# Turned tiles with PSUM banks of their own, wider turned blocks, and a new written order

## The chip, the cores and the metric

One core of one Trainium2 chip. The metric is the device time of one launch in microseconds (us), as the median of several runs; lower is better. The granted clock of TensorE was 1.00 of its upper level (2.4 GHz) in all but the last stretch of the profiled execution, where it was 0.98. Engines: PE (matrix engine), DVE (vector), ACT (scalar), POOL (GpSimd), SP (issues DMAs).

## The reference

Two sequences of 768 tokens go through three stages, all in fp32.

```
# 1. retention, 8 heads of 64, gamma_h = 1 - 2^(-5-h)
state = gamma * state + k_t v_t^T ;  y_t = q_t state / 8
# 2. layer norm and MLP, with residual, width 512 -> 2048 -> 512
xn = (x - mean) / sqrt(var + 1e-6) * g_ln
x  = x + relu(xn @ w_ch1) @ w_ch2
# 3. four experts' causal attention, head size 64
q, k, v = x @ wq[e], x @ wk[e], x @ wv[e]
a = softmax(causal(q k^T / 8));  ye = a @ v @ wo[e]
out = sum over the 2 experts with the largest x @ w_gate, softmax weight * ye
```

## The kernel before

**Tiles.** Retention works on 12 tiles of 128 tokens (2 sequences by 6). A tile needs: scores (`r_tile 2`, L581), the masked scores `am` on DVE (L587), the product with the old state (L600) and with the own values (L610), the update of the state in PSUM (L618), the scaling into `xT` in SBUF (DVE, L630), a turn of `xT` by eight 64x64 transposes against `ident` (`turn`, L422), statistics of that turned tile on DVE (L642 to L644) and POOL (L650, L651), the normed tile `xn` on ACT (L655), a second turn of `xn` (L422), and its copy on ACT (L664). The MLP works on stretches of 384 tokens. Each fp32 operand is split into a rounded high part and a low part, and a product takes three passes (high by high, high by low, low by high). First products stand at L766 and L858, second ones at L788; the residual is added into `xT` by DVE (L794, `m_c 2`). The last addition of a block is made in place in PSUM (L798, `m_c 3`), and ACT (L801, `m_c 4`) and DVE (L804, `m_c 5`) read that bank to split the result for stage 3. Attention takes pairs of 128-token query tiles: scores (L1047), a masked copy with its minimum on DVE (L1054), exponent with row sum on ACT (L1062), reciprocals on DVE (L1068, L1069), scaling on POOL (L1076), turns of the scaled rows `pr` in blocks of up to four 128-column slots (`a_turn`, L422), a copy of each block to `pt` or `ptn` on ACT or DVE (L446), the product with the values (L1117), its split (L1128, L1131), and the product with `wo` (L1144).

**PSUM.** The eight banks of 512 words are handed out by kind. A turned tile needs one strip of 256 words in each of two neighbouring banks, since the two halves of the array write to different banks. Two tiles share such a pair: `pb` (retention) has three pairs and `pc` (attention) two, each with two strips. Score banks (`ps1`) are the lower four and value banks (`psa`) the upper four.

**Order.** Nothing is scheduled at run time. Every step is a node with a cost per engine, the buffers that it needs and the keys that it reads and writes. `Plan.issue` lets a simulated clock run: an engine that is free takes, among the nodes whose inputs are there and whose buffers fit, the one with the lowest `prio`, which is the node's place in the program plus a number from the table `RANK`. On PE it adds `SWITCH` when a node has another form than the one before. A form is the part of the array that a matmul uses: whole (128 by 128, most products), rows (turns, scores), columns (L610, L618, L1117) and quarters (L600). The order that comes out is written down for each engine. On the chip an instruction then waits only for the semaphores of its inputs and of the bank it writes.

Of the kernel before, what the change touches and what calls it, by code (L numbers as in the profile page):

```python
# [48 lines left out]
SWITCH = 0.125  # L49
LAST = 10000  # L50
FILL = 12
TWO = ("pb", "pc")
# [6 lines left out]
WORDS = 205 * KB  # L59
# [6 lines left out]
class Buf:  # L66
# [96 lines left out]
class Plan:  # L163
# [43 lines left out]
    def issue(self):  # L207
# [18 lines left out]
        def strips(kind, off):  # L226
            return (off, off + 512) if kind in TWO else (off,)

# [82 lines left out]
def retention_channel_mlp_mixture_attention(ctx: ExitStack, tc: tile.TileContext, a):  # L311
# [114 lines left out]
    def new(n):  # L426
        return Buf(PL[n], n)
# [888 lines left out]
```

## Time and profile before

| | us |
|---|---|
| median of 3 runs (441.46 to 441.79) | 441.74 |
| profiled execution, whole | 442.45 |
| its span on the core | 440.7 |
| PE busy | 429.4 |
| DVE busy | 309.8 |
| ACT busy | 217.7 |
| POOL busy | 212.0 |

The page of the profile gives these busy times over the whole span. The span divides into retention with the first loads and the first MLP products (0 to 83 us), the dense MLP (83 to 305), and the rest of the MLP's additions with attention (305 to 441). A slice in which PE is busy all the time is bound by matmuls; only in the others can a change of order or of buffers move the end.

### The profile page before, as it was taken

To read this page: it belongs to the slowest core of one execution; us is meant where nothing else is said; L and a number is where in the kernel's file an instruction comes from. 1 tells how busy PE (TensorE), PEld (TensorE's weight loads), DVE (VectorE), ACT (ScalarE), POOL (GpSimd) and SP (SyncE) were. 2 spreads that over 40 slices of the span, in tenths; PEclk is the share of its full clock that TensorE was granted. 3 is DMA by queue.
4 is the path that set the end of the run, shared out by engine and by line. 5 is a ranking of instruction groups with operands and counts; after the bars stand their busy time and mean duration, and the time that the engine had idled before them with its cause. 6 is when DMAs were issued, how large, how long until landed. Compare 5 with 4: busy or idle time off the path is not lost.

```text
span 440.7 us, 9076 instructions
## 1 busy us (share of the span) xinstructions
PE 429.4 (97%) x3546; PEld 402.4 (91%) x3546; DVE 309.8 (70%) x743; ACT 217.7 (49%) x460; POOL 212.0 (48%) x219
## 2 busy tenths in 40 slices
PE   9988999999999999999999999999999999999996
PEld 8877889999999999999999999999999877887765
DVE  2769978765778876868877655668556778667663
ACT  1568775342656346335353264234533666656552
POOL 2668865999999528117136054200401343422430
PEclk9999999999999999999999999999999999999999
DMA  8999432210322304104112002001100001001121
GB/s 288 328 337 345 133 109 84 97 49 1 106 86 92 101 0 143 50 1 136 54 59 88 1 1 96 1 0 55 48 1 1 1 12 39 2 0 49 50 97 49
DMA packets 11995, 35.18 MB, mean 80 GB/s; under 512 B 1840, under 2 KB 2480, under 8 KB 11952
## 3 DMA queue, kind: packets, MB, share of 16 engines
q1 hardware_dynamic: 11952, 34.60, 22.7%
q8 instruction: 28, 0.46, 0.4%
q14 instruction: 15, 0.12, 0.1%
HBM read 31.45 MB, written 3.15 MB: 79 GB/s over the span
## 4 chain that ended last, share of the span: by engine, by line
PE 90%; ACT 3%; DVE 2%; DMA 2%; POOL 1%; issue 1%; SPq 0%; POOLq 0%; DVEq 0%
PE ps L788 30%; PE ps L858 20%; PE ps L766 8%; PE ps L952 8%; PE ps L1117 4%; PE ps L976 4%; PE ps L422 4%; PE ps L1144 4%; PE ps L1047 3%; DMA raw<-in_w_dram 2%; PE ps L529 2%; PE ps L610 1%; PE ps L581 1%; ACT xn L655 1%; PE ps L600 1%
## 5 line engine op out<-in xcount | busy, mean ns | idle before, releaser
L788 PE MATMUL ps<-h,w 128*128 128x384 f32 x768 | 142.4, 335 | 0.0
L788 PEld LDWEIGHTS ps<-h,w 128*128 128x128 f32 x768 | 133.7, 188 | 0.7 <-DVE ps L798 0.3
L794 DVE TENSOR_TENSOR xT<-xT,ps 128x384 f32<-128x384 f32 x112 | 60.2, 550 | 30.6 <-PE ps L788 30.1
L1076 POOL TENSOR_SCALAR pr<-pr,sm,gate 128x384 f32<-128x384 f32 (+5 forms) x48 | 34.0, 718 | 77.9 <-DVE sm L1069 34.1
L719 POOL TENSOR_TENSOR w<-wy,w 128x512 fp32r<-128x512 f32 x26 | 34.0, 1319 | 38.1 <-PE ps L788 23.4
L858 PE MATMUL ps<-t,S 128*128 128x384 f32 x216 | 42.1, 334 | 0.0
L858 PEld LDWEIGHTS ps<-t,S 128*128 128x128 f32 x216 | 37.8, 188 | 0.0
L1062 ACT ACTIVATE pr<-pr,sm 128x384 f32<-128x384 f32 (+5 forms) x48 | 31.7, 663 | 9.9 <-DVE sm L1054 9.9
L766 PE MATMUL ps<-x,w 128*128 128x384 f32 x192 | 35.2, 337 | 0.0
L877 ACT ACTIVATE h<-ps 128x384 fp32r<-128x384 f32 x36 | 17.7, 490 | 32.9 <-PE ps L788 20.6
L766 PEld LDWEIGHTS ps<-x,w 128*128 128x128 f32 x192 | 33.2, 188 | 0.3
L685 ACT ACTIVATE wx<-raw 128x512 f32<-128x512 f32 x32 | 21.5, 671 | 23.8 <-DVE ps L692 16.0
L687 POOL TENSOR_SCALAR wx<-wx 128x512 f32<-128x512 f32 x32 | 20.0, 625 | 23.9 <-ACT wx L685 23.0
L867 ACT ACTIVATE u<-ps 128x384 f32<-128x384 f32 x36 | 17.5, 488 | 25.3 <-PE ps L858 16.6
L858 PE MATMUL ps<-x,w 128*128 128x384 f32 x144 | 28.6, 334 | 0.0
L689 DVE TENSOR_SCALAR ps<-wx 128x512 uint32<-128x512 uint32 x32 | 22.0, 688 | 6.4 <-POOL wx L687 6.1
L858 PEld LDWEIGHTS ps<-x,w 128*128 128x128 f32 x144 | 25.3, 188 | 0.0
L1054 DVE CUSTOM_DVE_ANT_0 pr<-ps,mask 128x384 f32<-128x384 f32 (+4 forms) x48 | 22.1, 495 | 3.2 <-PE ps L1047 2.2
L695 DVE SCALAR_TENSOR_TENSOR wy<-raw,ps 128x512 uint32<-128x512 uint32 x32 | 21.8, 683 | 2.3 <-POOL w L719 1.7
L879 DVE SCALAR_TENSOR_TENSOR h<-ps,h 128x384 fp32r<-128x384 f32 x36 | 19.4, 551 | 5.3 <-ACT h L877 5.2
L692 DVE SCALAR_TENSOR_TENSOR ps<-wx,ps 128x512 uint32<-128x512 uint32 x32 | 22.2, 695 | 1.1
L587 DVE TENSOR_TENSOR am<-ps,caus 128x512 f32<-128x512 f32 x24 | 15.5, 683 | 9.9 <-PE ps L581 9.9
(122 smaller groups left out, 822.7 us busy)
## 6 DMA issues: line engine op xcount, KB each, us to landing
raw<-in_w_dram SPq DMA_DIRECT2D x32, 512.0 KB, 3.4
kq<-in_kq_dram SPq DMA_DIRECT2D x11, 512.0 KB, 5.1
vk<-in_vk_dram SPq DMA_DIRECT2D x9, 512.0 KB, 5.5
out_dram<-ob SPq DMA_DIRECT2D x11, 256.0 KB, 2.0
vk<-in_vk_dram SPq DMA_DIRECT2D x4, 256.0 KB, 3.8
vraw<-in_wv_dram SPq DMA_DIRECT2D x1, 520.0 KB, 3.9
kq<-in_kq_dram SPq DMA_DIRECT2D x2, 256.0 KB, 5.2
mraw<-in_wk_dram SPq DMA_DIRECT2D x1, 512.0 KB, 4.6
```

The costliest lines, as they stand in the source:

```text
L689: DVE(0.69, lambda: dve.tensor_scalar(u32(z), u32(x), 4, 1, op0=OP.logical_shift_left, op1=OP.logical_shift_right), r=[x], w=[z])
L692: DVE(0.7, lambda: dve.scalar_tensor_tensor(u32(z), u32(x), 0x80000000, u32(z), op0=OP.bitwise_and, op1=OP.bitwise_or), r=[x, z], w=[z])
L695: DVE(0.7, lambda: dve.scalar_tensor_tensor(u32(y), words(0), 29, u32(z), op0=OP.logical_shift_right, op1=OP.bitwise_or), r=[raw, z], w=[y])
L719: POOL(1.3, lambda: pool.tensor_tensor(f32r(l), f32(y), f32(h), OP.subtract), r=[y, h], w=[l])
L766: pe.matmul(f32(pa, TB), lhsT=wt, rhs=blk(f32r(xt[b][j]))[:, k], start=(n == 0), stop=(n == 11))
L788: pe.matmul(f32(pa, TB), lhsT=wt, rhs=t, start=(n == 0), stop=(n == 5))
L794: DVE(0.55, lambda: dve.tensor_tensor(blk(f32(xt))[:, k], blk(f32(xt))[:, k], f32(pa, TB), OP.add), r=[pa] + [(xt, cc, w) for cc in range( ...
L858: pe.matmul(f32(pa, TB), lhsT=wt, rhs=t, start=(first and n == 0), stop=(n == 5), skip_group_check=True)
L952: pe.matmul(f32(pa, TB), lhsT=mw(n, lo, k, p * 128, (p + 1) * 128), rhs=blk(f32r(xt))[:, k], start=(i == 0), stop=(i == 11))
L1054: DVE(0.22 + wide * 1.04e-3, lambda ks=ks, n=n, z=z, SC=SC: dve.tensor_tensor_reduce(f32(PR[z])[:, ks], f32(SC[z])[:, :wide], f32(MASK)[:, ...
L1062: ACT(act_c(nk) + .18, lambda pr=pr, z=z: act.activation(f32(pr, nk), f32(pr, nk), AF.Exp, bias=f32(sm)[:, z:z + 1], scale=-1.0, accum_out ...
L1076: POOL(0.34 + nk * 0.84e-3, lambda pr=pr, z=z, e=e: pool.tensor_scalar(f32(pr, nk), f32(pr, nk), f32(sm)[:, 6 + z:7 + z], GT[b, j][:, cc, ...
```

## The change

1. The planner splits a node's cost on DVE, ACT and POOL into a time that occupies the engine (cost less `LEAD`) and a latency (raised by `LEAD`). Table `RANK` has new numbers throughout; two lines stand for it below.
2. A turned tile owns both banks of its pair. `pb` has three pairs, `pc` four; score and value banks may be any of the eight.
3. In `a_turn` a tile with more than four slots is cut into two blocks of half its slots. The last query group has 11 slots: 6 and 5 instead of 4, 4 and 3. The middle group keeps 4 and 3, the first keeps 3. There are 40 blocks instead of 48. The buffers for `pt` and `ptn` get more places, in an arena that grows from 205 to 219 KB a partition.
4. `m_c 3` writes the sum to `xT` in SBUF; `m_c 4` and `m_c 5` read it there, and `m_c 3` is the bank's last reader.
5. The state's update and its copy use one key for both sequences; the copy of the gate's logits waits for the copy of the values; the value products wait for the blocks that they read (`needs`).

```diff
+LEAD = {"V": 0.085, "A": 0.1, "G": 0.05}
-WORDS = 205 * KB
+WORDS = 219 * KB
-    "a_turn 1": (48, (-25, 61, -103, -6, -56, -34, -58, -87)),
+    "a_turn 1": (40, (-3, -7, -55, -149, -149, -17, -40, -33)),
...
-        n.eng = eng
+        n.eng = {e: c - LEAD.get(e, 0.0) for e, c in eng.items()}
-        n.lat = lat
+        n.lat = lat + max(LEAD.get(e, 0.0) for e in eng)
...
-    PL["psa"] = banks[4:][::-1]
-    PL["ps1"] = banks[:4]
+    PL["psa"] = banks[::-1]
+    PL["ps1"] = banks
-    PL["pb"] = [("P", 1024 * i + 256 * k, 256) for i in (1, 2, 3) for k in range(2)]
-    PL["pc"] = [("P", 1024 * i + 256 * k, 256) for i in (3, 2) for k in range(2)]
+    PL["pb"] = [("P", 1024 * i, 1024) for i in (1, 2, 3)]
+    PL["pc"] = [("P", 1024 * i, 1024) for i in (3, 2, 1, 0)]
...
-            PE(0.47, upd, form="columns", r=[(vk, 1), vs] + (["first"] if i == 1 else []), w=[(STATE, b)] + (["first"] if i == 0 else []))
+            PE(0.47, upd, form="columns", r=[(vk, 1), vs], w=[STATE])
...
-        DVE(0.55, lambda: dve.tensor_tensor(f32(pa, TB), f32(pa, TB), blk(f32(xt))[:, k], OP.add),
+        DVE(0.55, lambda: dve.tensor_tensor(blk(f32(xt))[:, k], f32(pa, TB), blk(f32(xt))[:, k], OP.add),
...
-        ACT(0.49, lambda: act.activation(blk(f32r(xh))[:, k], f32(pa, TB), AF.Copy),
+        ACT(0.49, lambda: act.activation(blk(f32r(xh))[:, k], blk(f32(xt))[:, k], AF.Copy),
...
-        DVE(0.55, lambda: dve.tensor_tensor(blk(f32r(xl))[:, k], f32(pa, TB), blk(f32(xh))[:, k], OP.subtract),
+        DVE(0.55, lambda: dve.tensor_tensor(blk(f32r(xl))[:, k], blk(f32(xt))[:, k], blk(f32(xh))[:, k], OP.subtract),
...
-            for s0 in range(0, len(slots), 4):
-                part = slots[s0:s0 + 4]
+            half = (len(slots) + 1) // 2 if len(slots) > 4 else len(slots)
+            for s0 in range(0, len(slots), half):
+                part = slots[s0:s0 + half]
...
-                   r=[VV[b, j0], VV[b, j0 + 1]] + [(pt, j0 // 2) for pt in (*PT, *also)], w=[av])
+                   r=[VV[b, j0], VV[b, j0 + 1]] + [(pt, i) for pt in (*PT, *also) for i in needs[j0]], w=[av])
```

The diff moves nearly every instruction. Three places show how. Lines of the changed kernel are three higher from L422 on and six higher from L1117 on.

The first is PE late in attention, of before: two turns of a `pr` row, the products of two `at` tiles with `wo`, and the next turns.

```order
L422 MATMUL ps<-ident,pr_4563 128x64 x2
L422 MATMUL ps<-ident,pr_4669 128x64 x2
L1144 MATMUL ps<-wo_3555,at_4712 128x512
L1144 MATMUL ps<-wo_3565,at_4712 128x512
L1144 MATMUL ps<-wo_3555,at_4712 128x512
L1144 MATMUL ps<-wo_3555,at_4781 128x512
L1144 MATMUL ps<-wo_3565,at_4781 128x512
L1144 MATMUL ps<-wo_3555,at_4781 128x512
L422 MATMUL ps<-ident,pr_4563 128x64 x2
L422 MATMUL ps<-ident,pr_4669 128x64 x4
```
The same engine some 30 rows earlier, of the changed kernel.

```order
L425 MATMUL ps<-ident,pr_4622 128x64 x2
L1150 MATMUL ps<-wo_3551,at_4630 128x512
L1150 MATMUL ps<-wo_3561,at_4630 128x512
L1150 MATMUL ps<-wo_3551,at_4630 128x512
L1150 MATMUL ps<-wo_3551,at_4668 128x512
L1150 MATMUL ps<-wo_3561,at_4668 128x512
L1150 MATMUL ps<-wo_3551,at_4668 128x512
L1150 MATMUL ps<-wo_3551,at_4630 128x512
L1150 MATMUL ps<-wo_3561,at_4630 128x512
L1150 MATMUL ps<-wo_3551,at_4630 128x512
L1150 MATMUL ps<-wo_3551,at_4668 128x512
L1150 MATMUL ps<-wo_3561,at_4668 128x512
```
Before, six `wo` products (whole array) stand between turns (rows). Now eleven of twelve are seen in one run, for the same two tiles; a turn follows the twelfth.

The second is the end of ACT's order, of before: the last exponents, the copies of the last turned blocks `pt`, and the last `at` and `ob`.

```order
L1128 ACTIVATE at_5091<-ps 128x256
L446 ACTIVATE pt_5102<-ps 128x2x4x64
L446 ACTIVATE pt_5102<-ps 128x2x3x64
L446 ACTIVATE pt_5128<-ps 128x2x4x64
L1128 ACTIVATE at_5157<-ps 128x128 x2
L446 ACTIVATE ob_5174<-ps 128x256
```
The end of ACT's order now.

```order
L449 ACTIVATE pt_4991<-ps 128x2x6x64
L449 ACTIVATE pt_5016<-ps 128x2x6x64
L449 ACTIVATE pt_5041<-ps 128x2x6x64
L449 ACTIVATE pt_5066<-ps 128x2x6x64
L1134 ACTIVATE at_5093<-ps 128x256
L1134 ACTIVATE at_5104<-ps 128x256
L1134 ACTIVATE at_5137<-ps 128x256
L1134 ACTIVATE at_5143<-ps 128x128 x2
```
The copies of the last group now carry six slots (128x2x6x64) instead of four and three; ACT's last exponent stands ahead of all of them, and the last copy to `ob` is not on ACT.

The third is PE in the middle of retention, of before: state updates (`vs,vk`), scores (`kq`), turns of `xT` and `xn`, products with the old state (`kq,sn`) and with the values (`am,vs`).

```order
L618 MATMUL ps<-vs_357,vk_265 64x64 x8
L581 MATMUL ps<-kq_292 128x128 x8
L422 MATMUL ps<-ident,xn_391 128x64 x8
L422 MATMUL ps<-ident,xT_189 128x64 x8
L600 MATMUL ps<-kq_231,sn_229 64x128 x8
L610 MATMUL ps<-am_373,vs_357 64x128 x4
L610 MATMUL ps<-am_379,vs_357 64x128 x4
L618 MATMUL ps<-vs_406,vk_322 64x64 x8
```
The same place of the changed kernel.

```order
L613 MATMUL ps<-am_300,vs_251 64x128 x4
L621 MATMUL ps<-vs_328,vk_271 64x64 x8
L584 MATMUL ps<-kq_244 128x128 x8
L425 MATMUL ps<-ident,xT_234 128x64 x8
L425 MATMUL ps<-ident,xn_322 128x64 x8
L425 MATMUL ps<-ident,xn_388 128x64 x8
L603 MATMUL ps<-kq_218,sn_288 64x128 x8
L613 MATMUL ps<-am_338,vs_328 64x128 x4
```
Three turns (one of `xT`, two of `xn`) now stand together, and each holds a pair of banks of its own from its turn to the end of the reading of it; before, a turn of `xn` and one of `xT` stood so.

## Rows read from the trace of the kernel before

**Rows 1.** Busy time by stage (length; busy of each engine; clock; DMA share; GB/s).

```profile
0.00:83.00 83.00, 78.05 (x1074) 70.14 (x1075) 60.64 (x138) 48.85 (x96) 54.31 (x71) 1.00 0.64 222
83.00:305.00 222.00, 222.00 (x1282) 221.76 (x1281) 160.66 (x288) 98.81 (x188) 118.23 (x98) 1.00 0.17 55
305.00:441.00 136.00, 129.38 (x1194) 110.47 (x1192) 88.51 (x319) 70.06 (x177) 39.46 (x51) 1.00 0.09 33
```
**Rows 2.** Chain that ended last (start us, us, what), one piece of the MLP.

```profile
82.86 8.33 PE ps L788 x48
```
**Rows 3.** Waits of PE (us in total, times, longest us).

```profile
PE ps L422 <- DVE pt L446: 1.6, 3, 0.7
PE ps L422 <- ACT xn L655: 1.2, 1, 1.2
PE ps L422 <- ACT xc L664: 1.1, 2, 0.6
...
PE ps L618 <- POOL vs L571: 0.8, 2, 0.4
PE ps L422 <- ACT ptn L446: 0.7, 2, 0.4
PE ps L422 <- DVE mv L642: 0.4, 1, 0.4
PE ps L422 <- DVE at L1131: 0.3, 1, 0.3
PE ps L422 <- DVE ptn L446: 0.2, 1, 0.2
```
**Rows 4.** Timeline of PE, retention (start us, us, instruction, matmuls, wait).

```profile
20.31 0.41 PE L422 MATMUL ps<-ident,xn 64*128 64x64 f32 x8
20.56 1.11 PE L581 MATMUL ps<-kq 64*128 64x128 f32 x16
...
29.76 0.46 PE L422 MATMUL ps<-ident,xT 64*128 64x64 f32 x8 [1.20 <-ACT xn L655]
...
52.81 0.46 PE L422 MATMUL ps<-ident,xn 64*128 64x64 f32 x8
53.20 2.37 PE L766 MATMUL ps<-x,w 128*128 128x384 f32 x12
55.49 0.67 PE L600 MATMUL ps<-kq,sn 64*64 64x128 f32 x16
```
**Rows 5.** Timeline of PE, the end of attention.

```profile
417.48 0.71 PE L422 MATMUL ps<-ident,pr 64*128 64x64 f32 x16
...
430.79 0.65 PE L422 MATMUL ps<-ident,pr 64*128 64x64 f32 x14 [0.41 <-DVE pt L446]
...
434.47 2.70 PE L1144 MATMUL ps<-wo,at 128*128 128x256 f32 x15
```
**Rows 6.** Instruction groups of the layer norm (busy us, mean ns, idle before).

```profile
L642 DVE BATCH_NORM_STATS2 mv<-ps 128x6 f32<-128x256 f32 x24 | 9.1, 422 | 4.2 <-PE ps L422 3.3 <-ACT xn L655 0.6
L650 POOL TENSOR_TENSOR mv<-mv,half 128x1 f32<-128x1 f32 x12 | 6.6, 549 | 3.4 <-DVE mv L644 3.0 <-POOL wx L687 0.2
L655 ACT ACTIVATE xn<-ps,mv 128x512 f32<-128x512 f32 x12 | 9.3, 776 | 7.6 <-POOL mv L651 6.0 <-issue 1.5
```
**Rows 7.** Instruction groups of the copies of turned blocks.

```profile
L446 DVE COPY pt<-ps 128x512 f32<-128x512 f32 x8 | 5.4, 690 | 3.5 <-ACT pt L446 3.5
L446 ACT ACTIVATE pt<-ps 128x512 f32<-128x512 f32 x8 | 4.8, 599 | 5.9 <-PE ps L422 5.9
L446 ACT ACTIVATE pt<-ps 128x384 f32<-128x384 f32 x5 | 2.4, 488 | 2.1 <-PE ps L422 1.6 <-DVE pt L446 0.4
```
**Rows 8.** Instruction groups that split results, and one weight of POOL.

```profile
L804 DVE TENSOR_TENSOR x<-ps,x 128x384 fp32r<-128x384 f32 x16 | 8.6, 551 | 0.9 <-ACT x L801 0.6
L879 DVE SCALAR_TENSOR_TENSOR h<-u,h 128x384 fp32r<-128x384 f32 x12 | 10.3, 861 | 0.0
L925 POOL TENSOR_TENSOR wo<-mraw,wo 128x1024 fp32r<-128x1024 f32 x1 | 2.4, 2395 | 33.5 <-PE ps L952 33.5
```

More of the change, by code (lines that the diff above doesn't have):

```diff
@@ L49 @@
 SWITCH = 0.125
+LEAD = {"V": 0.085, "A": 0.1, "G": 0.05}
 LAST = 10000
 FILL = 12
-TWO = ("pb", "pc")
 COLD = 6.0
@@ L218, in fits @@
                 for o in live.get(sp, ()):
-                    if (o.users or o.end > t) and any(x < y + size and y < x + o.at[2] for x in strips(o.kind, o.at[1])
-                                                      for y in strips(b.kind, off)):
+                    if (o.users or o.end > t) and o.at[1] < off + size and off < o.at[1] + o.at[2]:
                         break
@@ L224, in fits @@
             return None
-        def strips(kind, off):
-            return (off, off + 512) if kind in TWO else (off,)
         for n in self.nodes:
@@ L364, in retention_channel_mlp_mixture_attention @@
     o_u = o_sm + 2 * KB
-    assert o_u + 3 * KB // 2 * 3 <= WORDS
+    o_z = o_u + 3 * KB // 2 * 3
+    assert o_z + 14 * KB <= WORDS
     x = o_r
@@ L398, in retention_channel_mlp_mixture_attention @@
     PL["pr"] = region(o_xt, 3 * KB, 8) + region(o_h + 24 * KB, 3 * KB, 4)
-    PL["pt"] = region(o_x, 6 * KB, 3)
-    PL["ptn"] = region(o_x, 7 * KB // 2, 5) + region(o_r + 24 * KB, 7 * KB // 2, 3)
+    PL["pt"] = region(o_x, 6 * KB, 3) + region(o_z, 6 * KB, 2) + region(o_x + 24 * KB, 6 * KB, 4)
+    PL["ptn"] = region(o_x, 7 * KB // 2, 5) + region(o_r + 24 * KB, 7 * KB // 2, 3) + region(o_z, 7 * KB // 2, 4) + region(o_x + 24 * KB, 7 * KB // 2, 6)
     PL["at"] = region(o_x + 18 * KB, 2 * KB, 3)
@@ L406, in retention_channel_mlp_mixture_attention, with two @@
     PL["ps"] = banks[::-1]
-    PL["psa"] = banks[4:][::-1]
-    PL["ps1"] = banks[:4]
+    PL["psa"] = banks[::-1]
+    PL["ps1"] = banks
     PL["state"] = banks[:1]
-    PL["pb"] = [("P", 1024 * i + 256 * k, 256) for i in (1, 2, 3) for k in range(2)]
-    PL["pc"] = [("P", 1024 * i + 256 * k, 256) for i in (3, 2) for k in range(2)]
-    def two(b):
-        i, k = divmod(b.at[1], 1024)
-        return ps[:, 1024 * i:1024 * i + 1024].rearrange("p (h c) -> p h c", h=2)[:, :, k:k + 256]
+    PL["pb"] = [("P", 1024 * i, 1024) for i in (1, 2, 3)]
+    PL["pc"] = [("P", 1024 * i, 1024) for i in (3, 2, 1, 0)]
+    def two(b, n=256):
+        return view(b).rearrange("p (h c) -> p h c", h=2)[:, :, :n]
     def turn(dst, n, src):
@@ L421, in turn @@
                 hs = slice(64 * h, 64 * h + 64)
-                pe.transpose(two(dst)[:, h, i * 64:i * 64 + 64], src(i)[hs], ident[hs, hs])
+                pe.transpose(two(dst, 64 * n)[:, h, i * 64:i * 64 + 64], src(i)[hs], ident[hs, hs])
     P = Plan()
@@ L621, in r_tile @@
             P.at = "r_tile 6"
-            PE(0.47, upd, form="columns", r=[(vk, 1), vs] + (["first"] if i == 1 else []), w=[(STATE, b)] + (["first"] if i == 0 else []))
+            PE(0.47, upd, form="columns", r=[(vk, 1), vs], w=[STATE])
             sn = SN[b] = SNB[b][c % 2]
             P.at = "r_tile 7"
-            ACT(0.38, lambda: act.activation(f32(sn)[:, :NP * D], state(b), AF.Copy), r=[(STATE, b)], w=[sn])
+            ACT(0.38, lambda: act.activation(f32(sn)[:, :NP * D], state(b), AF.Copy), r=[STATE], w=[sn])
         xt = XT[b][j]
@@ L797, in m_c @@
         P.at = "m_c 3"
-        DVE(0.55, lambda: dve.tensor_tensor(f32(pa, TB), f32(pa, TB), blk(f32(xt))[:, k], OP.add),
-            r=[pa, (xt, "k", k)] + [(xt, cc, w) for cc in range(TPB) for w in range(2)], w=[pa])
+        DVE(0.55, lambda: dve.tensor_tensor(blk(f32(xt))[:, k], f32(pa, TB), blk(f32(xt))[:, k], OP.add),
+            r=[pa, (xt, "k", k)] + [(xt, cc, w) for cc in range(TPB) for w in range(2)], w=[(xt, "k", k)])
         P.at = "m_c 4"
-        ACT(0.49, lambda: act.activation(blk(f32r(xh))[:, k], f32(pa, TB), AF.Copy),
-            r=[pa], w=[(xh, "k", k)] + (keys(xh) if k == 0 else []))
+        ACT(0.49, lambda: act.activation(blk(f32r(xh))[:, k], blk(f32(xt))[:, k], AF.Copy),
+            r=[(xt, "k", k)], w=[(xh, "k", k)] + (keys(xh) if k == 0 else []))
         P.at = "m_c 5"
-        DVE(0.55, lambda: dve.tensor_tensor(blk(f32r(xl))[:, k], f32(pa, TB), blk(f32(xh))[:, k], OP.subtract),
-            r=[pa, (xh, "k", k)], w=[(xl, "k", k)] + (keys(xl) if k == 0 else []))
+        DVE(0.55, lambda: dve.tensor_tensor(blk(f32r(xl))[:, k], blk(f32(xt))[:, k], blk(f32(xh))[:, k], OP.subtract),
+            r=[(xt, "k", k), (xh, "k", k)], w=[(xl, "k", k)] + (keys(xl) if k == 0 else []))
     TH = [[Buf(PL["t"], "t") for _ in range(4)] for b in range(B)]
@@ L987, in q_val @@
         P.at = "q_val 3"
-        DVE(0.2, lambda: dve.tensor_copy(f32(g)[:, cc * E:(cc + 1) * E], f32(pa, n)[:, E * HD:]), r=[pa], w=[(g, cc)])
+        DVE(0.2, lambda: dve.tensor_copy(f32(g)[:, cc * E:(cc + 1) * E], f32(pa, n)[:, E * HD:]), r=[pa, v], w=[(g, cc)])
     for b in range(B):
@@ L1099, in a_turn @@
                 COPY(n * C, lambda pt=pt, s0=s0, n=n: f32(pt)[:, s0 * C:(s0 + n) * C].rearrange("p (n h c) -> p h n c", n=n, h=2),
-                     lambda pa=pa, n=n: two(pa)[:, :, :n * 64].rearrange("p h (n c) -> p h n c", n=n),
-                     [pa], [(pt, s0 // 4)])
+                     lambda pa=pa, n=n: two(pa, n * 64).rearrange("p h (n c) -> p h n c", n=n),
+                     [pa], [(pt, s0 // half)])
         return PT
@@ L1105, in a_value @@
         nj = 2 * g + 2
+        half = (0, 4, 6)[g]
+        needs = {j0: sorted({min((2 * j0 + i) // half, 1) if half else 0 for i in (0, 3)}) for j0 in range(0, nj, 2)}
         avs, at = [new("psa") for _ in range(2 if last else 1)], new("at")
@@ L1306 @@
     arrays = {f"in_{n}_dram": x for n, x in _layouts(**inputs).items()}
-    nc = _bacc.Bacc("TRN2", target_bir_lowering=False, num_devices=1)
+    nc = _bacc.Bacc("TRN2", target_bir_lowering=False, num_devices=1, dynamic_dma_scratch_size=1024)
     aps = {}
```

145 rows, old and new, of the table RANK are left out of this document.

## Prediction, made before the changed kernel ran

> **What bounds the kernel now.** I read the stages first, then the chain that ended last, then the waits of PE, and last PE's timeline at the places with waits. In the stages [rows 1] the reader is to see that PE is busy for all of the 222 us between 83 and 305, for 78.05 of the first 83 and for 129.38 of the last 136, while DVE, ACT and POOL have room in each. So PE bounds everything. Its work there is one unbroken chain: 48 products of 384 columns take 8.33 us, 0.1735 each [rows 2]. The change adds and removes no matmul, so these 222 us stay. What can change lies in the first and the last stage and has two parts. One is PE's waits [rows 3]. Without the start these are 3.5 us in retention (1.2 for `xn`, 1.1 for `xc`, 0.8 for `vs`, 0.4 for `mv`) and 2.8 in attention (1.6, 0.7, 0.3, 0.2 for copied blocks and `at`), 6.3 in all. The other part counts as busy and shows only in the timeline: a group of matmuls that uses another part of the array than the one before starts late [rows 4]. Twelve whole-array products starting at 53.20 need 12 x 0.1735 = 2.08, but the next group (quarters) starts 2.29 after them, which is 0.21 lost. The turn at 52.81 gives way to the whole array after 0.39, where the turn at 20.31 gives way to scores, which have the same form, after 0.25: 0.14 lost. Out of the whole array and back costs 0.35, or 0.17 a change. For changes among the smaller forms I take 0.10, an estimate between nothing and that 0.17.
>
> **The change, part by part.** First, the order on PE. I counted changes of form in the order as written, before against now. Up to the end of the early stage there are 16 with the whole array on one side and 34 others before, and 22 and 27 now: 6 x 0.17 - 7 x 0.10 = +0.3 us. In attention there are 42 and 9 before, 22 and 12 now: -20 x 0.17 + 3 x 0.10 = -3.1. The printed place with twelve `wo` products in one run instead of six between turns is one of those twenty. The sum is -2.8. With the others at nothing or at 0.17 it is -2.4 or -3.1, so the count is not sensitive to my choice; what is uncertain is whether all of it was on the path. Where PE would have waited for a copy anyway, a saved 0.17 only lengthens the wait.
>
> Second, the banks in retention. A turned tile occupies its pair from the turn (0.25) through two statistics of 0.42, the power of 0.55 and the normed copy of 0.78 [rows 6], at least 2.4 us; with the small instructions and semaphores between I take 3.5 for the first of a tile's two turns and somewhat over 1 for the second. Tiles follow each other every 3.4 us or so (12 in some 41 us of PE work, the end of retention being mixed with the MLP). That fills three pairs to about half, but in lumps, as the printed place with three turns in a row shows; a fourth turn there, or a score bank that lies in the same pair, would have to wait for an `xn`. Before, two tiles could share a pair, but then the pair was lost to scores until both had left. Following the new order with these durations I find a wait of about 0.3 a tile, 12 x 0.3 = 3.6, against 3.5 before: no change. The ends of the unknown are no waits there (-3.5) and the longest wait of the trace, 1.20 for an `xn` [rows 4], at most tiles, which is the first rival.
>
> Third, the blocks of a turn. Eight turned blocks fewer means eight copies fewer; but each of six slots moves 768 columns, which no row shows. From 384 to 512 columns ACT goes from 0.49 to 0.60 [rows 7], 0.11 for 128 columns, so 768 is 0.82 on ACT, an estimate; DVE's 512 takes 0.69, and 768 by the same steps about 0.95. A product of values that waits for a whole block waits 0.2 to 0.25 longer, but no longer has a third block to wait for. DVE and ACT have 35% and 48% of the last stage free [rows 1], so the copies themselves are hidden; bounds are a loss of 0.25 at each of the four largest pairs of blocks, +1.0, and a gain of as much.
>
> Fourth, the waits of attention. Before, the turns wait for a place, because a pair is handed out again only after its copy ([rows 5], 0.41 at 430.79; queued behind it on PE are the value products and the last `wo` products). Now there are four pairs, and score banks can come from all eight, but 0.1 to 0.2 is due where scores follow turns onto banks just released. Walking through the new order I find 0.4 for three such places, 0.25 and 0.2 for a turn and a value product behind softmax, 0.4 for two scores that wait for banks, 0.5 for the last turns (the scores before them are 5.5 us of PE work earlier and their softmax needs 5.1), and 0.45 for the last `at` before the final `wo` products: 2.2 against 2.8, -0.6. Bounds: all gone, -2.8; or twice as long as I think, +1.6.
>
> Fifth, `m_c 3` to `m_c 5`. With both inputs in SBUF the subtraction may be slower than 0.55 [rows 8]: the like instruction on `h<-u` takes 0.86 in the mean, 0.31 more. 16 x 0.31 = 5.0 if each were on the path. But the first product that reads the last split block has 3.1 us of PE work in front of it and the chain from the sum to the split is about 2, so 1 us of slack hides it; I count nothing. A gain is as little to be had, since PE waits for none of these banks now. If that cover went, each of the four groups would show one 0.31, +1.2.
>
> Here a page of the notes speaks against the change. The Trainium skill, "SBUF — State Buffer", section "Who interferes with whom", says that a VectorE instruction with two SBUF inputs contends with a GpSimd instruction that reads SBUF. The group of `h<-u` agrees with it: its mean is 0.86 where the like subtraction with one input in PSUM has 0.55 [rows 8]. By it one subtraction could stand still for a whole weight split of POOL, 2.4, and the sum would be up to 1.4 higher where that falls on the last block of a group, whose slack is 1; without it the sum stays.
>
> Sixth, the rest. The state's single key puts the two sequences' updates in turn, which the order already does; the gate's copy behind the values' copy is work on DVE that no product waits for; SP issues the same loads with two halves earlier. Together nothing, within 0.5 either way. The final copy and store after the last `wo` products [rows 5] keep their 3.5 us.
>
> **Sum.** The profiled execution took 442.45, 0.71 more than the median of the runs. 442.45 - 2.8 + 0 - 0.6 = 439.05; less 0.71 it is 438.3 against 441.74.
>
> **Rivals.** (a) Slower: banks of their own stall retention. If eight of twelve tiles wait as long as the tile at 29.76, 1.20 each, retention's waits are 9.6 instead of 3.5: 441.74 - 3.4 + 6.1 = 444.4. It decides when they pass 6.9 us. For it speaks that a turn behind an `xn` is the longest wait already and that three turns now stand in a row; against it, that DVE, POOL and ACT are at 73, 65 and 59% in that stage [rows 1], so that a tile's chain is seldom late by much. (b) No change: the saved form changes fall into waits. Scores now stand in longer runs, and DVE must copy each before its bank is free; seven places at 0.41 [rows 5] are 2.9, which leaves 441.74 - 3.4 + 2.9 = 441.2. For it speaks that DVE is the busiest of the helpers; against it, that it has 35% free there. (c) More: the freer banks halve the waits of both stages, 6.3 to about 3: 441.74 - 2.8 - 3.3 = 435.6. For it speaks that all but the start of PE's waits are on a copy or a bank; against it, that retention gets fewer strips. (d) The subtraction from SBUF is on the path after all, every one of 16 at +0.31: 441.74 - 3.4 + 5.0 = 443.3. Against it stands the 1 us of slack; some part of it is possible, all of it hardly.
>
> **How the numbers follow.** Forecast 438.3, with a range of its own from 436.3 to 440.5: 0.55. Rival (a) 0.12, (b) 0.12, (c) 0.16, (d) 0.05. A measurement of this kernel can tell from no change about 0.2%, 0.9 us; faster is below 440.86 and slower above 442.62. Forecast and (c) are faster, 0.71, and a little of (b) and (d), 0.03; most of (b) and the nearest of (a) are the same, 0.11; the rest of (a) and (d) is slower, 0.15. The range for 8 in 10 goes from 434.8, half of (c)'s lower side left out, to 442.4, where (b) is inside and most of (a) is not.
>
> **What would show it.** Right: PE's busy time falls by 2 to 3 us with the same count of matmuls, nearly all of it after 305 us; between 83 and 305 the unbroken stretch keeps its length; PE's waits stand at 5.5 to 6; the subtraction at its new line takes 0.55 to 0.9 and no product waits for it; ACT's copies of 768 columns take about 0.8. Wrong: waits of turns for `xn` or `xc` above 7 us in retention (a), scores waiting for DVE's masked copies (b), first products of stage 3 waiting for the subtraction (d), or a PE busy time that has not fallen, which would mean that a change of form costs less than its two neighbours at 53 us say.

## The result and the profile after

The changed kernel takes 444.86 us (median of 4 runs, 444.74 to 446.06) against 441.76: 1.0075 times as long, 95% interval 1.0054 to 1.0095. That is 3.1 us slower, where 3.4 us faster was forecast, and outside the range. The profiled execution took 444.74, its span is 442.9 (before 440.7).

The stages first, as in [rows 1] (length; busy time of PE, PEld, DVE, ACT, POOL; clock; DMA).

```profile
0.00:83.00 83.00, 78.60 (x1074) 70.55 (x1075) 62.13 (x142) 46.28 (x86) 53.78 (x71) 1.00 0.65 228
83.00:305.00 222.00, 217.53 (x1245) 215.19 (x1244) 157.77 (x272) 94.84 (x184) 120.02 (x100) 1.00 0.16 53
305.00:443.00 138.00, 132.82 (x1231) 117.14 (x1230) 97.38 (x328) 70.75 (x177) 39.30 (x51) 1.00 0.09 32
```
The reader is to see the second row: PE is busy for 217.53 of the 222 us in which it was busy throughout before. So 4.5 us are lost where the prediction saw nothing to lose, and the clock is 1.00 in all three. To place the rest I summed, in both traces, for each group of like matmuls the time from its first start to the next group's first start, less their number times the spacing at which their kind runs (0.1733 us for 384 columns). I call this lost time. For the short kinds its size depends on the spacing taken; the difference between the two kernels hardly does, since both run the same matmuls. From 83 to 305 us it is 0.23 before and 6.62 after. Up to 83 us it rises by 0.1, and after 305 it falls by 4.7. The sum of the three is 1.8, and the last matmul ends 1.78 later. So the first stage came out even, attention gained 4.7, and the MLP lost 6.4.

PE's waits, as in [rows 3] (total, times, longest).

```profile
PE ps L791 <- DVE h L776: 2.4, 1, 2.4
PE ps L584 <- DMA kq<-in_kq_dram: 1.5, 2, 0.9
...
PE ps L791 <- DVE h L882: 1.0, 1, 1.0
PE ps L979 <- issue: 0.7, 1, 0.7
PE ps L425 <- ACT xn L658: 0.6, 1, 0.6
PE ps L603 <- DVE am L590: 0.6, 1, 0.6
...
PE ps L861 <- DVE xT L797: 0.5, 1, 0.5
PE ps L791 <- DVE xT L797: 0.5, 2, 0.3
PE ps L1050 <- ACT ptn L449: 0.3, 1, 0.3
PE ps L425 <- DVE am L590: 0.2, 1, 0.2
PE ps L1050 <- DVE pt L449: 0.2, 1, 0.2
```
The waits of retention and attention that stood there before are nearly gone: turns wait 0.8 us for `xn` and `am`, where three lines of L422 in retention had 2.7, and attention has 0.5 where it had 2.8. New in retention are 1.5 for loads of `kq` and 0.6 for `am`, so that all its waits are 2.9 where they were 3.5. New are also waits of the MLP's products for DVE: 2.4 for `h` at L776, 1.0 for `h` at L882, 1.0 for `xT`. The MLP's waits are 4.4 of its 6.4. Most of the other 2.0 stands behind them: after each, the product that waited and the next one come some 0.27 us later than the listed wait and the usual spacing give, and the profile counts that as busy.

The timeline of all engines around the longest wait (start us, us, engine, instruction, wait) shows what DVE did.

```profile
114.45 0.76 POOL L713 TENSOR_TENSOR w<-wy,w 128x256 fp32r<-128x256 f32 x1
...
114.76 4.43 DVE L738 TENSOR_TENSOR sf<-wy,wy 128x256 f32<-128x256 f32 x1 [0.24 <-ACT wy L704]
115.14 0.76 POOL L738 TENSOR_TENSOR sf<-wy 128x256 f32<-128x256 f32 x1
...
115.84 1.32 POOL L722 TENSOR_TENSOR w<-wy,w 128x512 fp32r<-128x512 f32 x1
...
116.27 0.49 ACT L774 ACTIVATE h<-ps 128x384 fp32r<-128x384 f32 x1
117.09 1.82 POOL L830 TENSOR_TENSOR t<-t,t 128x768 fp32r<-128x768 f32 x1
119.12 0.55 DVE L776 SCALAR_TENSOR_TENSOR h<-ps,h 128x384 fp32r<-128x384 f32 x1
...
119.72 0.45 PE L791 MATMUL ps<-h,w 128*128 128x384 f32 x1 [2.45 <-DVE h L776]
```
DVE begins the first weight sum `sf`, 256 columns with both inputs in SBUF, at 114.76, and is done 4.43 us later. POOL meanwhile runs four instructions without a gap, the last until 118.91; DVE's sum ends 0.28 us after that. Behind it in DVE's queue is the split `h` (L776). Its input, the ACT copy at 116.27, was there at 116.76, but it starts at 119.12 and PE's next product at 119.72. The second sum, later and alone, takes 0.41. In the kernel before the first sum and POOL's neighbours of it read as follows.

```profile
112.68 1.09 DVE L735 TENSOR_TENSOR sf<-wy,wy 128x256 f32<-128x256 f32 x1 [0.98 <-ACT wy L701]
112.70 0.79 POOL L710 TENSOR_TENSOR w<-wy,w 128x256 fp32r<-128x256 f32 x1
...
113.40 0.97 POOL L735 TENSOR_TENSOR sf<-wy 128x256 f32<-128x256 f32 x1
```
There it waited for one POOL instruction and took 1.09, although POOL's next one is recorded from before the former's end. Two more places after, at 157 and at 321 us, show the same with one POOL instruction each.

```profile
157.15 2.39 POOL L743 TENSOR_TENSOR S<-sf,S 128x1024 fp32r<-128x1024 f32 x1 [1.17 <-ACT S L741]
157.48 2.48 DVE L882 SCALAR_TENSOR_TENSOR h<-u,h 128x384 fp32r<-128x384 f32 x1
...
160.01 0.62 PE L791 MATMUL ps<-h,w 128*128 128x384 f32 x2 [0.96 <-DVE h L882]
```
The split `h<-u` ends 0.42 after POOL's low part of S, and PE waits 0.96 for it. The other is one of the splits that the change moved to SBUF (`m_c 5`).

```profile
321.39 2.42 POOL L928 TENSOR_TENSOR wv<-vraw,wv 128x1040 fp32r<-128x1040 f32 x1
321.61 2.62 DVE L807 TENSOR_TENSOR x<-xT,x 128x384 fp32r<-128x384 f32 x1 [0.59 <-ACT x L804]
...
325.27 1.68 PE L979 MATMUL ps<-wv,x 128*128 128x260 f32 x12 [0.68 <-issue]
```
It stands still beside POOL's split of `wv` (2.62 against 0.55 elsewhere), and PE's next value product starts 0.68 late, which the profile puts down to issue. The two go together: in the runs a_c, a_d, a_e, a_f and a_sf_pool below this split took 2.63 to 2.79 and the product waited 0.7 or 0.8; in a_again, a_hold, a_both and a_d2 it took its usual time and the wait was not there. The groups (busy us, mean ns, idle before):

```profile
L882 DVE SCALAR_TENSOR_TENSOR h<-u,h 128x384 fp32r<-128x384 f32 x12 | 12.7, 1055 | 0.5 <-ACT h L880 0.3
L807 DVE TENSOR_TENSOR x<-xT,x 128x384 fp32r<-128x384 f32 x16 | 10.7, 682 | 2.8 <-ACT x L804 2.4
```
Before, the twelve `h<-u` had a mean of 861 ns and the sixteen last splits 551 [rows 8]; now it is 1055 and 682. The new copies of 768 columns take 0.81 on ACT and 0.95 on DVE, as estimated.

Such meetings are not new. In the kernel before, seven of the twelve `h<-u` took 0.55 to 0.56 and five, each beside POOL, 1.03 to 1.64. The longest stood beside POOL's split of `wq` (276.12 to 278.52):

```profile
277.30 1.64 DVE L879 SCALAR_TENSOR_TENSOR h<-u,h 128x384 fp32r<-128x384 f32 x1
```
PE waited for none of them: between 83 and 305 us it had no wait. What is new is how long the longest are, and that one of PE's next products hangs on them.

### The profile page after: what moved, and what is told of

It is laid out like the page before. It is cut to its first block, busy times and chain, and to the rows that moved or that the text cites. A ratio compares the mean times of both kernels' runs of the same rounds, so it can differ in the third digit from the quotient of the medians.

```text
span 442.9 us, 9056 instructions
## 1 busy us (share of the span) xinstructions
PE 429.0 (97%) x3546; PEld 402.9 (91%) x3546; DVE 317.3 (72%) x741; ACT 211.9 (48%) x445; POOL 213.1 (48%) x222
## 4 chain that ended last, share of the span: by engine, by line
PE 79%; DVE 9%; DMA 4%; ACT 3%; POOL 2%; issue 2%; SPq 1%; DVEq 0%; ACTq 0%; POOLq 0%
PE ps L791 26%; PE ps L861 17%; PE ps L955 8%; PE ps L769 6%; PE ps L1050 4%; PE ps L1123 4%; PE ps L425 4%; PE ps L1150 3%; PE ps L979 3%; DMA kq<-in_kq_dram 3%; DVE h L882 2%; DMA raw<-in_w_dram 2%; PE ps L584 1%; PE ps L613 1%; DVE sf L738 1%
## 5 line engine op out<-in xcount | busy, mean ns | idle before, releaser
L791 PE MATMUL ps<-h,w 128*128 128x384 f32 x768 | 144.1, 336 | 4.0 <-DVE h L776 2.4
L1079 POOL TENSOR_SCALAR pr<-pr,sm,gate 128x512 f32<-128x512 f32 (+5 forms) x48 | 33.8, 720 | 65.2 <-DVE sm L1071 40.9
L882 DVE SCALAR_TENSOR_TENSOR h<-ps,h 128x384 fp32r<-128x384 f32 x36 | 19.9, 553 | 12.0 <-ACT h L880 11.9
```

What stands on the lines that cost most here:

```text
L791: pe.matmul(f32(pa, TB), lhsT=wt, rhs=t, start=(n == 0), stop=(n == 5))
L882: DVE(0.55, lambda: dve.scalar_tensor_tensor(f32r(l, TB), f32(src, TB), 0.0, f32(h, TB), op0=OP.max, op1=OP.subtract), r=[src, h], w=[l])
L1079: POOL(0.34 + nk * 0.84e-3, lambda pr=pr, z=z, e=e: pool.tensor_scalar(f32(pr, nk), f32(pr, nk), f32(sm)[:, 6 + z:7 + z], GT[b, j][:, cc, ...
```

## The experiments

**Theory 1**: DVE instructions with two inputs in SBUF stand still while POOL reads SBUF; the new order puts several of them beside POOL's long work and right ahead of something PE needs. **Theory 2**: the helpers' queues are too full in the new order, and a long sum is only where that shows. All edits of the changed kernel but a_norank leave its planned order as it is and act where the order is written down. Beside each set of kernels the kernel before ran on the same chip; its median there was 442.0 to 442.3, so ratios are what is compared.

**The two sums on POOL (a_sf_pool).**

```diff
         for n, e in order:
+            if n.at in (("w_sums 1", 0), ("w_sums 1", 1)):
+                e = "G"
             n.fn(e)
```

> The changed kernel, its order unchanged, but the first two of the four weight sums sf (L738) of the first seven-product piece are issued on POOL in place of DVE. Theory 1 (DVE is locked out by POOL): the sum took 4.43 us on DVE instead of some 0.4 to 0.7 because POOL ran four instructions on SBUF back to back, and the split h (L776) queued behind it came 2.45 us late for PE at 119.7 us. Then that wait falls to under 0.5 us, PE's idle time in the MLP falls by about 2.2, and the time is about 442.6. Theory 2 (the helpers' queues are too full in the new order, and the long sum is only where that shows): the inputs of the split are late as well, the wait moves on to the next split, and less than 0.7 us is won: 444.2 to 444.9.

Measured: 444.88, ratio 1.0052 (1.0032 to 1.0072), no gain in the median and none beyond the intervals in the ratio. The wait for `h` is gone, as theory 1 has it, but another is there (timeline):

```profile
122.15 4.10 DVE L745 TENSOR_TENSOR S<-sf,S 128x1024 fp32r<-128x1024 f32 x1 [2.22 <-ACT S L743]
...
123.35 1.82 POOL L822 TENSOR_TENSOR t<-x,x 128x768 f32<-128x768 f32 x1
...
126.31 0.97 PE L863 MATMUL ps<-t,S 128*128 128x384 f32 x4 [2.08 <-DVE S L745]
```
The next DVE instruction with two SBUF inputs, the low part of S (1.65 in the changed kernel), now falls among POOL's, takes 4.10, and PE waits 2.08 for it. The time is the one that theory 2 gave. But the input of the split was not late, and the new wait is another DVE instruction that stands still beside POOL, which is theory 1's mechanism: the stall moved along the queue. This run alone does not decide between the two.

**Two POOL instructions held behind the split (a_hold).** A one-column copy on POOL that reads the split's result is put ahead of the long instruction.

```diff
+HOLD = ((('w_sums 3', 1), ('m_h7 5', 7)), (('load_mw 3', 1), ('m_h7 5', 39)))
...
+            if n.at in held:
+                self.touch(self.made[held[n.at]])
             n.fn(e)
```

> The changed kernel, but two long POOL instructions (the low part of S at 157 us and the low part of wq at 280 us) are put behind the DVE split h<-u that they overlapped, by a one-column POOL copy that reads h. Theory 1: the two splits take 0.55 to 0.7 us instead of 2.48 and 1.80, PE's waits of 0.96, 0.31 and 0.17 us behind them go, and the time falls by 1.2 to 1.5 us to about 443.5. Theory 2: the splits are late for other reasons, the waits stay within 0.5 us, and the time is 444.5 or more, since POOL is now later too.

Measured: 442.82, ratio 0.9999 (0.9973 to 1.0025). The waits behind both splits are gone; the one at 158 us takes 0.55. More was won than expected; in the profile the sum `sf`, whose order and neighbours were not touched, this time got in:

```profile
114.39 0.74 POOL L728 TENSOR_TENSOR w<-wy,w 128x256 fp32r<-128x256 f32 x1
114.70 0.70 DVE L753 TENSOR_TENSOR sf<-wy,wy 128x256 f32<-128x256 f32 x1 [0.24 <-ACT wy L719]
...
115.08 0.93 POOL L753 TENSOR_TENSOR sf<-wy 128x256 f32<-128x256 f32 x1
```
It took 0.70, with POOL's own sum beside it at 0.93 instead of 0.76. What is left of PE's waits in the MLP:

```profile
PE ps L877 <- DVE xT L812: 1.8, 1, 1.8
```
The 1.8 is behind `h<-u` at 136 us, which took 1.68 beside POOL; before the edit PE had come there later and waited 0.5.

**Both, and the place at 137 us (a_both).** The sums go to POOL as above, and one more pair is held:

```diff
-HOLD = ((('w_sums 3', 1), ('m_h7 5', 7)), (('load_mw 3', 1), ('m_h7 5', 39)))
+HOLD = ((('x_sums 4', 5), ('m_h7 5', 3)), (('w_sums 3', 1), ('m_h7 5', 7)), (('load_mw 3', 1), ('m_h7 5', 39)))
```

> The changed kernel with both of the former edits and one more: the POOL difference t at 136.5 us is also put behind the split h<-u at 137.25 (1.48 us). Theory 1: of PE's 6.6 us lost in the MLP some 4.3 go (2.45, 0.51, 0.96, 0.31, 0.17, less what moves), and the time is about 440.5, below the kernel before, because attention lost 4.7 us less than before. Theory 2: under 1.5 us is won, 443.4 or more.

Measured: 443.47, ratio 1.0028 (1.0005 to 1.005), 2.1 us under the changed kernel by the ratios (1.0075 less 1.0028 of 442). Theory 1's 440.5 was missed by 3 us, and the time is theory 2's. The wait list of the MLP:

```profile
PE ps L879 <- DVE S L760: 2.1, 1, 2.1
PE ps L879 <- POOL t L848: 1.0, 1, 1.0
```
The first is the low part of S again (4.12). The second is the price of the hold: PE needed the difference `t` 1 us before it came.

**Part 4 alone in the kernel before (b_part4).** The order is the old one.

```diff
-            dve.tensor_tensor(f32(pa, TB), f32(pa, TB), blk(f32(xt))[:, k], OP.add)
+            dve.tensor_tensor(blk(f32(xt))[:, k], f32(pa, TB), blk(f32(xt))[:, k], OP.add)
...
-            dve.tensor_tensor(blk(f32r(xl))[:, k], f32(pa, TB), blk(f32(xh))[:, k], OP.subtract)
+            dve.tensor_tensor(blk(f32r(xl))[:, k], blk(f32(xt))[:, k], blk(f32(xh))[:, k], OP.subtract)
```

> The kernel before, its order unchanged, with part 4 of the change alone: the last residual is written to xT in SBUF, and the split reads it there (ACT L801, DVE L804 with two inputs in SBUF). Theory 1: DVE's split may meet POOL's split of wo and wv (some 2.4 us each at 312 to 317) and stand still up to 2.4 us; 0 to 0.7 us reach PE: 441.7 to 442.4. The prediction's step (slack hides it): 441.7, within 0.2%. Against both: every one of the 16 slower by 0.3 us on the path, 443 or more.

Measured: 442.07, ratio 0.9991 (0.9974 to 1.0008): no difference. Not one of the splits is slower:

```profile
L804 DVE TENSOR_TENSOR x<-xT,x 128x384 fp32r<-128x384 f32 x16 | 8.6, 552 | 1.0 <-ACT x L801 0.6
```
In the old order they stand before and after POOL's `wo` and `wv`, none beside them. So the prediction's "I count nothing" holds for the edit, and the price comes from where the order puts it.

**Five places at once (a_c, a_d and a_d2).** The low part of S is kept clear by holding POOL's next instruction behind it, the pairs at 157 and 280 us are held as above, the split at 137 us is issued after the two additions that PE waited for; in a_c the two sums are on POOL, in a_d they stay on DVE and POOL's own sum and difference are held behind them. The place at 321 us is left as it is. a_d2 is a_d once more beside the changed kernel. Of a_d:

```diff
+HOLD = ((('w_sums 1', 2), ('w_sums 1', 0)), (('x_sums 4', 3), ('w_sums 1', 1)), (('split_piece 2', 13), ('w_sums 3', 0)),
+        (('w_sums 3', 1), ('m_h7 5', 7)), (('load_mw 3', 1), ('m_h7 5', 39)))
+SWAP = ((('m_h7 5', 3), ('m_c 2', 33)),)
```

> The changed kernel with the meeting points of DVE and POOL in the MLP taken apart one by one: the first two sums sf on POOL; the POOL instruction after the long difference at 121 us put behind DVE's low part of S, which took 4.10 us when sf had been moved; the low parts of S (157 us) and wq (280 us) put behind the split h<-u; and that split at 137 us issued after the two additions into xT that PE waited for. Theory 1 (a DVE instruction with two SBUF inputs stands still until POOL's queue leaves a gap): the low part of S takes 1.7 to 2.4 us, no wait of PE between 83 and 305 us is over 0.5 us, their sum is under 1.5 us, and the time is 440 to 441.2, less than the kernel before by 1 us or more. Theory 2 (queues too full, waits only move): a wait of 1 us or more shows up elsewhere and the time is 443 or more.

> As the former, but the two sums sf stay on DVE, and it is POOL that is held: its own sum behind DVE's first, its long difference t behind DVE's second. Theory 1: the first sum takes under 1.0 us in place of 4.43, the second under 1.8, PE's wait of 2.45 us for the split h (L776) is gone, and the time is 440 to 441.5. Theory 2: the sum is slow on DVE for a reason of its own (its operands), stays over 2 us, and the time is 443 or more.

> The version with all five meeting points taken apart (the run a_d) again, beside the changed kernel on one chip. Theory 1: 3 to 3.5 us below the changed kernel, 441.4 to 441.9, within 0.2% of the kernel before.

Measured: a_c 441.63, ratio 0.9996 (0.9987 to 1.0005); a_d 441.64, 0.999 (0.9971 to 1.0009); a_d2 441.68, 0.9983 (0.9969 to 0.9997), where the changed kernel beside it (a_again) has 1.0042 (1.0022 to 1.0062). In a_d2 the sum takes 0.73, the low part of S 1.76, the split at 139 us 0.78, and the MLP's waits of PE are

```profile
PE ps L813 <- DVE xT L819: 0.6, 1, 0.6
PE ps L884 <- POOL t L853: 0.3, 1, 0.3
PE ps L884 <- DVE xT L819: 0.3, 1, 0.3
PE ps L884 <- ACT u L893: 0.2, 1, 0.2
```
1.4 us in all, where from 83 to 345 us the changed kernel had 5.1 in its first profile and 3.9 in a_again. That is 2.5 us back by medians side by side (444.22 to 441.68, where 3 to 3.5 were expected), and 3.2 by the medians of two different sets (444.86 to 441.64). a_d2 is the only version whose interval lies below both kernels, and by little: 0.03 to 0.31% under the kernel before, which a_c and a_d could not tell from none. For these five places theory 2 is out, since the queues hold the same work. The time of 440 to 441.2 that theory 1 gave was missed by half a microsecond.

Not all of the MLP's loss is back. Summed as above, its lost time is 4.8 in a_c, 4.2 in a_d and 4.5 in a_d2, against 6.6 in the changed kernel and 0.2 in the kernel before. So the five places are worth some 2 of the 6.4 us, and the versions are level with the kernel before only because attention's 4.7 stand against the rest. What is left are the short waits above, the late starts behind them and gaps too short for the wait list. No run takes these away, and whether the helpers' fuller queues are behind them is open.

**One place alone (a_f) and the changed kernel again (a_again).** a_f has the two holds at the sums only, a_again no edit.

```diff
+HOLD = ((('w_sums 1', 2), ('w_sums 1', 0)), (('x_sums 4', 3), ('w_sums 1', 1)))
```

> The changed kernel once more, without any edit, on the same chip as the next two. It tells whether the long sum sf (4.43 us) belongs to this program or came up once. Theory 1 as first put (DVE stands still until POOL leaves a gap) expects 4 us or more again, PE's wait of about 2.4 for h, and 444.9. If DVE gets in by chance, the sum may take 0.7 to 1.1 here, and the time is then 442.5.

> The changed kernel with two holds alone: POOL's own sum is put behind DVE's first sum sf, and POOL's long difference t behind DVE's second. Theory 1: sf takes at most 1 us, PE's wait of 2.45 us for h goes, the places at 137, 157, 281 and 321 us stay as they are, and the time falls by 1.8 to 2.4 us against the changed kernel of the same call, to about 442.7, unless DVE's low part of S then meets POOL (4.1 us as when sf was moved), which takes the gain back. Theory 2: less than 0.7 us.

Measured: a_again 444.22; the sum is as long as the first time:

```profile
114.83 4.43 DVE L738 TENSOR_TENSOR sf<-wy,wy 128x256 f32<-128x256 f32 x1 [0.24 <-ACT wy L704]
```
The products behind the long wait differ, though. This is PE's timeline there, first of the changed kernel's first profile, then of a_again, and the stretch from 120 to 123 us of a_again as in [rows 1]:

```profile
119.72 3.42 PE L791 MATMUL ps<-h,w 128*128 128x384 f32 x18 [2.45 <-DVE h L776]
119.79 4.98 PE L791 MATMUL ps<-h,w 128*128 128x384 f32 x18 [2.44 <-DVE h L776]
120.00:123.00 3.00, 3.00 (x10) 3.00 (x10) 2.00 (x5) 1.06 (x1) 2.86 (x3) 0.50 0.00 0
```
In a_again the granted clock was at its lower level (0.50 of the upper one, so 1.2 GHz), and the same 18 products took 1.56 us longer. It had fallen after PE had stood for 2.44 us; after the same wait in the first profile it stayed at 1.00. In a_hold it fell too, behind the wait of 1.8 us. Of the twelve executions of a_again eight have a mean granted clock of 0.995 or 0.996 and a median of 444.63; the other four have 443.14. None of the 36 executions of a_c, a_d and a_d2 is below 0.998. So some 1 us of the 2.5 that a_d2 is faster than a_again goes with the clock, an estimate from these medians; only the profiled executions show where it fell, and the kernel before has such executions as well (4 of the 25 in this set).

a_f 444.59, ratio 1.006 (1.0034 to 1.0086). The sums take 0.73 and 0.44 and PE's wait of 2.4 is gone, yet no time is won. The waits left:

```profile
PE ps L878 <- DVE xT L813: 1.9, 1, 1.9
PE ps L807 <- DVE h L899: 1.0, 1, 1.0
```
PE, no longer 2.4 us late, meets the split at 136 us earlier and waits 1.9 for the additions behind it (0.5 before). Theory 1's gain for one place was wrong, and the time is theory 2's again: a stall gives slack to the next. Of the versions here those paid that took all five places apart, and a_hold, in which the sum got in by itself.

**Without the table (a_norank, b_norank).** One execution of each kernel.

```diff
-RANK = {
...
+RANK = {}
```

> The changed kernel with an empty table RANK, so that the planner orders by program place alone. With the next one it tells what the structure (own banks, wider blocks, wider choice of score and value banks) gives without a table. If the structure brings attention's gain, PE's lost time after the MLP is 3 us or more below that of the next kernel. If the table brings it, the two are within 1.5 us there. No forecast of the whole time: without a table both are some 5 to 20 us slower than with one, an estimate from nothing but the size of PE's loss (20.7 us) in the tuned orders.

> The kernel before with an empty table RANK: the counterpart of the former.

Measured: 467.76 with the change, 458.02 without. From the first scores of stage 3 on, PE's lost time, summed as above, is 0.6 longer with the change. That includes a stretch of 3.4 us at the lower clock (424 to 427 us, after a wait of 0.67), worth up to 1.7, so the structure alone may have given attention some 1.1, an estimate; most of the gain of 4.7 came with the new order. From 83 us to the first scores, the MLP and the projections, it is 8.8 longer with the change, of which two more such stretches are up to 3.4. Here the moved split is dear (timeline):

```profile
328.24 2.40 POOL L850 TENSOR_TENSOR wo<-mraw,wo 128x1024 fp32r<-128x1024 f32 x1 [32.72 <-ACT wo L848]
328.56 5.17 DVE L729 TENSOR_TENSOR x<-xT,x 128x384 fp32r<-128x384 f32 x2 [0.17 <-ACT x L726]
```
Two of them take 5.17 us beside POOL's `wo` and `wv`, and the first projections behind wait 2.7.

**A train on POOL in the kernel before (b_train, b_memset).** After POOL's difference beside DVE's first sum come four copies of it (below), or in b_memset twelve writes of zeros by `pool.memset(filled, 0.0)`.

```diff
             n.fn(e)
+            if n.at == ("split_piece 8", 0):
+                for _ in range(4):
+                    n.fn(e)
```

> The kernel before, its order unchanged, but the POOL difference of 0.75 us (L710) that stands beside DVE's first weight sum sf (L735, 1.09 us there) is issued five times in a row with the same result, so that POOL reads SBUF for some 3.7 us without a gap. Theory 1 (DVE with two SBUF inputs stands still until POOL's queue leaves a gap): the sum takes 3 to 4.5 us, as it did in the changed kernel, or, if it gets in between two of them, about 1.1; the work queued behind it on DVE is late by as much and PE waits for the split h, 0.5 to 2 us. Theory 2 (DVE only ever waits for the one POOL instruction that runs): at most 1.2 us for the sum, and no wait of PE for h. POOL's own work is 3 us later under both, which may by itself cost PE up to about 1 us, an estimate.

> The same place, but in place of four more differences POOL writes zeros twelve times to a place that nobody reads (128x160 each), which reads nothing from SBUF. Theory 1 with reading as its condition: the sum sf stays at 0.4 to 1.1 us, though POOL is as busy. If any POOL work holds DVE off, the sum takes 2 us or more.

Measured: b_train 444.66, ratio 1.0055 (1.0035 to 1.0075). The sums got in at once:

```profile
111.50 1.09 DVE L738 TENSOR_TENSOR sf<-wy,wy 128x256 f32<-128x256 f32 x1 [0.98 <-ACT wy L704]
111.58 4.12 POOL L713 TENSOR_TENSOR w<-wy,w 128x256 fp32r<-128x256 f32 x5
...
113.02 0.46 DVE L738 TENSOR_TENSOR sf<-sf,wy 128x256 f32<-128x256 f32 x1
```
1.09 and 0.46, though POOL had five instructions in a row. But these five stand 0.08 us apart in the trace, while in the changed kernel the second, third and fourth of POOL's four each begin 0.06 to 0.07 before the recorded end of the one ahead. So this train does not test "stands still until the queue leaves a gap". Against that rule speak the kernel before and a_hold, where the sum got in between POOL instructions without a gap. The time lost goes with POOL's later work (PE waits 0.4 for its `w` and 0.7 for DVE's `wy`; the MLP's lost time is 2.6). b_memset 444.42, ratio 1.0048 (1.0029 to 1.0066):

```profile
115.58 0.42 DVE L740 TENSOR_TENSOR sf<-sf,wy 128x256 f32<-128x256 f32 x1
```
The second sum is at its full speed among writes (0.42), as theory 1 has it, but as it was 0.46 among reads, this run tells little.

**An earlier load (a_e).** On the base of a_d.

```diff
-SWAP = ((('m_h7 5', 3), ('m_c 2', 33)),)
+SWAP = ((('m_h7 5', 3), ('m_c 2', 33)), (('load 4', 3), ('load 1', 4)))
```

> The version with POOL held behind DVE's two sums sf, the low part of S and the splits h<-u, and one more edit: on SP the load of kq that retention's fifth scores waited for (1.2 us at 15.6 us) is issued ahead of the load of vk before it. Theory 1 holds the MLP's losses to be paid back already, so what is left is the start: 0.5 to 1.2 us of that wait go, and the time is 440.5 to 441.2, 0.1 to 0.3% under the kernel before. If the load is not what decides, the time stays at 441.6.

Measured: 442.42, ratio 0.9998 (0.9974 to 1.0022). The waits for `kq` fell from 1.7 in a_d (1.2 in a_d2, the same program) to 1.0, waits for `xn` and `vs` took their place, and the time did not fall.

## Why the prediction was wrong

The step that failed is in its first part: "The change adds and removes no matmul, so these 222 us stay." It rests on the sentence ahead of the prediction that only in slices where PE is not busy all the time a change of order can move the end, and that is wrong: it moved most in the others. PE had been busy there throughout, but only since every split and sum of the helpers came in time, the stalled ones too; the helpers' orders are new, and I costed them for retention and attention alone. The MLP lost 6.4 us where nothing stood, which by itself is nearly the whole distance between forecast and result (438.3 and 444.86). The runs with five places taken apart bring 2.5 us back side by side, where the changed kernel was 1.9 slower than the kernel before. Of the MLP's own 6.4 they bring back some 2; what cost the rest is open. The like rule was in my hands, and I put it and the row of `h<-u` against `m_c 5` only, not against the 12 splits `h<-u` and the sums `sf` that the new order moved.

The Trainium skill, "SBUF — State Buffer", section "Summary: rules for kernel authors", says that where VectorE has two SBUF inputs and a GpSimd instruction reads SBUF, the second one to issue blocks until the first has finished. The trace agrees with it at 157 and 321 us (2.48 beside 2.39, 2.62 beside 2.42); the 4.43 us across four instructions are more than it says.

Point by point:
- Form changes: -2.8 forecast. After 305 us the lost time fell by 4.7; the waits there fell from 2.8 to 1.1, with the 0.7 behind the split at 321 us, so 3.0 are left, where -3.1 stood. That fits, but no run shows place by place that it was the form changes. In the first stage the groups that change from or to the whole array lost some 2 us more, 0.6 of it a wait for a load, where +1.0 stood; the others gained as much. PE's busy time fell by 0.5, not by 2 to 3, because 2.0 of new busy time stand in the MLP, behind its waits.
- Banks in retention: no change forecast, by 3.6 us of waits for 3.5. The stage came out even, by luck: of 2.9 us of waits turns have 0.8 and `am` 0.6, and 1.5 are loads of `kq`, to which the prediction's sixth part gave nothing. Rival (a), the slower one by which the range was closed, is out.
- Blocks of a turn: the two estimates of a copy were right, and they are hidden.
- Attention's waits: -0.6 forecast, -2.3 measured. Rival (c) had the right sign there, and (b) is out.
- `m_c 5`: nothing was right for the edit (b_part4). In the new order one split of sixteen meets `wv` in some executions and costs 0.7: rival (d) at one place.
- The end result, slower by 3.1, is that of no rival: (a) gave +2.7 from another place.

What stays open is why the same sum took 4.43 in two profiles of the changed kernel and 0.70 in a_hold, with POOL's first instruction begun 0.30 to 0.31 us ahead of it in each, and 1.09 in b_train. It was not tried to set the two engines' starts apart by a known time.

## What to carry to other kernels

An engine that is busy without a gap is not safe from a reordering: ask, for each instruction that it waits for, what now stands ahead of it on the helper, and whether that can be held up by a third engine. Where an order is planned from costs per engine, instructions of DVE and POOL that hold each other up need a joint cost, or a planned order that looks denser runs slower. And repair such places together: here, taking one away alone (a_sf_pool, a_f) won nothing, since PE then ran into the next.

## What the runs showed of the hardware that was not expected

A 256-column sum on DVE, 0.41 us by itself, took 4.43 us while POOL ran four instructions back to back, and a 1024-column one 4.10 in place of 1.65 to 1.93 (4.12 in a second run). The same sum took 0.70 and 1.09 beside POOL in other programs. So such an instruction may be passed over several times, not once. In the profiles of the kernel before, the changed kernel, a_hold and b_train the first sum ended 0.28 or 0.29 us after the end of a POOL instruction; why it is one and not the one ahead of it, no run settles. For the sum it was the same in two executions of one program; for the split at 321 us it differed between executions of one program (2.62 and its usual 0.55).

A wait of PE costs more than the profile lists: some 0.27 us in the two products behind it. After a wait of 2.44 us the granted clock once fell to its lower level, which cost 1.56 us more, and in another execution of the same program it did not.
